# Expert outputs of the large tiles transposed by VectorE and scaled on ScalarE, in a fused FFT-convolution and mixture-of-experts kernel

## The chip, the cores and the metric

The kernel runs on one core of a Trainium2 chip. The metric is the device time of one launch in microseconds. Three runs of the kernel before took 2051.51, 2045.4 and 2051.67 us (median 2051.51). The profiled execution is another run: 2045.59 us, of which 2043.8 lie between its first and last instruction (the span).

Engine names in the rows: PE is TensorE (PEld its weight loads), DVE is VectorE, ACT is ScalarE, POOL is GpSimd, SP is SyncE, which here only issues DMAs. PEq, SPq, ACTq and POOLq are the sequencers of these engines.

## The reference

A causal convolution of every channel along the sequence by FFT, then a top-1 mixture of experts on the 45,568 rows that it gives:

```python
def _attn_ref(x, h):                      # x (8, 5696, 128), h (5696, 128)
    L = 2 * S
    Yf = np.fft.rfft(x, n=L, axis=1) * np.fft.rfft(h, n=L, axis=0)[None, :, :]
    return np.fft.irfft(Yf, n=L, axis=1)[:, :S, :].astype(np.float32)

def _moe_ref(x, modality_id, w_gate, modality_bias, w1, w2):   # 8 experts, 128 -> 1024 -> 128
    logits = x @ w_gate + modality_bias[modality_id]
    e_idx = np.argmax(logits, axis=1)
    probs = softmax(logits); gate_w = probs[np.arange(N), e_idx]
    for e in range(E):
        mask = e_idx == e
        h = np.maximum(x[mask] @ w1[e], 0.0)
        out[mask] = gate_w[mask, None] * (h @ w2[e])
```

## The kernel before

**Convolution.** `stage1` and `stage23` do the forward transform and the product with the filter in two groups of four batches; `stage4` does the last part of the inverse transform, computes the gate's logits and the place of each row in its expert's region, and puts (index, rows) on a queue. `dispatch` takes from that queue and GpSimd scatters 128 rows at a time to `rows_d` in device memory (L320): 128 values, the gate weight and the row's number in the output, 130 words a row. Each expert has its own region there.

**Expert tiles.** `Moe.tiles` works through 104 jobs: 81 large tiles of 512 rows (levels 0, 1 and 2 with 18, 18 and 45 tiles) and 23 small ones of 256 rows (level 3), the last three only if a count read on the chip asks for them; in the profiled run it didn't. Three weight slots are loaded from `w12s` when the expert of a slot changes (2 MB each, L613). A large tile has eight steps f, a small one four. Each step t, f does:
- `gemm1`: three matmuls of 512 columns (high and low parts of weights and rows), ScalarE's Relu into `hh` (L647), VectorE's rest into `hl` (L648);
- `gemm2`, two steps later (LAG = 2): three matmuls that add into `po`. With the last one, ScalarE copies `po` to `ot` (L669).

`load` (L603, L605) brings rows and their gate weight and row number (`mrt`, `mmt`) for the tile three ahead; for large tiles `mrt` comes in four DMAs with runs of 128 bytes, so that a VectorE transpose of 32x32 blocks (L626) completes the turning of the rows. `prep` makes the high and low parts (L629, L630) for the next tile at f = 4. `finish`, at f = 2 of the next tile, turns `ot` back: four TensorE transposes into the single bank `pxt` (L677), then VectorE multiplies with the gate weight into `of` (L680). The bank `pxt` also serves the transposes of the rows of small tiles (L622).

**Output.** 128 rows go out in one GpSimd scatter (a piece, L709). Tiles of levels 0 and 1 run while GpSimd is needed for `dispatch`; their outputs go to `late_d` (one DMA with rows of 2 KB, L684), and their row numbers are copied by GpSimd to `held` (L683). From tile 37 on, `bring` loads them again (L694). Pieces of levels 2 and 3 go out from `of` directly. `evenly` lets out at most one piece a step, 0.883 a step on the mean, each tied to that step's Relu; fresh pieces (`outs`) go ahead of brought ones (`backs`). What is left after the last tile is let out without a pace.

**Order.** While convolution and tiles run side by side (to about 1340 us), a scheduler sets the order on all engines but SP. In the last part, where tiles run alone (`alone`), TensorE's order is that of the code as well; ScalarE, VectorE and GpSimd keep the scheduler's. DMAs of SP and ACT take eight completion semaphores in turn: a DMA is issued only after the one eight places before it has landed.

**Tables.** `level` works out from the counts on which rows and expert each tile works. Level 2 and 3 are made together after the last `dispatch`; before them SP writes a padding of 512 rows behind each expert's region (L829).

Of the kernel before, what the change touches and what calls it, by code (L numbers as in the profile page):

```python
# [22 lines left out]
E, FF = 8, 1024  # L23
# [38 lines left out]
NHELD = LEVELS[0] + LEVELS[1]  # L62
SMALL = LEVELS[3] - NLAST
EVEN = ((NHELD + LEVELS[2]) * NSUB + SMALL * TSL // 128) / (8 * (LEVELS[2] - 2) + 4 * (SMALL - 3))
# [27 lines left out]
def conv_moe(  # L92
# [234 lines left out]
    def stage4(g, sp, ps, psl, qa, qb, paced=False, late=None):  # L327
# [39 lines left out]
        for q0 in range(qa, qb, QB):  # L367
# [7 lines left out]
            for qi in range(QB):  # L375
# [32 lines left out]
                else:  # L408
                    ys = [late.tile([128, GB, 128], BF16, name=f"ys{i}") for i in range(3)]
# [97 lines left out]
    def table(tp, lv, before):  # L507
# [26 lines left out]

        cnt = u_(E, "cnt")
# [8 lines left out]
        for s in range(3):  # L544
            nc.vector.tensor_tensor(sums[:, s + 1, E:], sums[:, s, E:], sums[:, s, E - (1 << s):2 * E - (1 << s)], op=ALU.add)
        cum = sums[:, 3, E - 1:]
# [8 lines left out]
        nc.vector.scalar_tensor_tensor(val[:, 1:], cum[:, :E], float(-ts), cur, op0=ALU.mult, op1=ALU.add)  # L555
        dlt = u_(E, "dlt")
# [3 lines left out]
        nc.vector.tensor_reduce(rb, ge, axis=AX.X, op=ALU.add)  # L560
        tmp = u_(nt, "tmp")
# [16 lines left out]
    class Moe:  # L578
        def __init__(self, wp, sp0, sp, pst, psh, pso):
# [3 lines left out]
            self.outs = []  # L583
            self.tabs = {}
            self.held = wp[0].tile([128, NHELD, NSUB], I32, name="held")
            self.back, self.backs, self.credit = 0, [], 0.0
# [4 lines left out]
        def load(self, t):  # L591
# [6 lines left out]
            mt = self.sp0.tile([128, NSUB, 2], F32, name="mmt", bufs=5)  # L598
# [6 lines left out]
            nc.sync.dma_start(mt[:, :ns], src[bass.ds(r0, ts), D:].rearrange("(c p) w -> p c w", p=128))  # L605
# [9 lines left out]
        def prep(self, t):  # L615
            st = self.st[t]
            rt, ts, ns = st["rt"], st["ts"], st["ns"]
            xp, s = (self.sp, "") if t else (self.sp0, "0")
            if self.on_pe(t):
# [3 lines left out]
                pf = px.rearrange("p c t -> p (c t)")[:, :ts]  # L623
            else:
                pf = self.sp0.tile([128, TS], F32, name="mxt", bufs=1)[:, :ts]
                nc.vector.transpose(pf, rt[:, :ts])  # L626
            xh = xp.tile([128, TS], F32R, name="mxh" + s)
            xl = xp.tile([128, TS], F32R, name="mxl" + s)
            nc.scalar.copy(xh[:, :ts], pf)  # L629
            nc.vector.tensor_tensor(xl[:, :ts], pf, xh[:, :ts].bitcast(F32), op=ALU.subtract)  # L630
            st.update(xh=xh[:, :ts], xl=xl[:, :ts])
# [19 lines left out]
        def gemm2(self, t, f):  # L651
# [15 lines left out]
            if k == 7:  # L667
                ot = self.sp.tile([128, TS], F32, name="ot")
                nc.scalar.copy(ot[:, :ts], po)  # L669
                st["ot"] = ot  # L670

        def finish(self, t):
            st = self.st.pop(t)
            ns = st["ns"]
            pq = self.pst.tile([128, NSUB, 128], F32, name="pxt")
            for c in range(ns):
                nc.tensor.transpose(pq[:, c, :], st["ot"][:, c * 128:(c + 1) * 128], ident)  # L677
            of = self.sp.tile([128, NSUB, D], F32, name="of")
            rt = st["mt"]
            nc.vector.tensor_tensor(of[:, :ns], pq[:, :ns], rt[:, :ns, 0:1].to_broadcast([128, ns, D]), op=ALU.mult)  # L680
            ri = rt.bitcast(I32)
            if t < NHELD:
                nc.gpsimd.tensor_copy(self.held[:, t, :].unsqueeze(2), ri[:, :, 1:])  # L683
                nc.sync.dma_start(late_d[t], of.rearrange("p c d -> p (c d)"))  # L684
                return
# [3 lines left out]
        def bring(self):  # L689
            if self.back < NHELD and len(self.backs) <= NSUB // 2:  # L690
                t = self.back
                self.back += 1
                of = self.sp.tile([128, NSUB, D], F32, name="ob")
                nc.sync.dma_start(of.rearrange("p c d -> p (c d)"), late_d[t])  # L694
                for c in range(NSUB):
                    self.backs.append((t, c, self.held[:, t, c:c + 1], of))
# [27 lines left out]
        def tiles(self, first, total):  # L724
# [11 lines left out]
            for g in range(len(steps) + LAG):  # L736
# [5 lines left out]
                if t < total:  # L742
# [3 lines left out]
                    if t > NHELD:  # L746
                        self.bring()
# [173 lines left out]
```

## Time and profile before

| | |
|---|---|
| runs | 2051.51, 2045.4, 2051.67 us |
| profiled execution | 2045.59 us, span 2043.8 us |
| TensorE busy | 1962.4 us, 96% |
| VectorE busy | 1445.8 us, 71% |
| ScalarE busy | 1133.6 us, 55% |
| GpSimd busy | 1112.3 us, 54% |

Four stages follow one another: the transforms up to about 800 us; the end of the inverse transform beside the tiles of levels 0 and 1 up to about 1340; large tiles alone up to about 1902; small tiles to the end. Busy time is the time in which at least one record of an engine is open. Matmuls overlap (one record of 512 columns lasts 0.39 us and the next begins 0.23 us after it), so the start-to-start distance, not the mean duration, tells what one costs.

### The profile page before, as it was taken

What the parts mean: (1) busy time and instruction counts of PE and PEld (TensorE: products, weight loads), DVE (VectorE), ACT (ScalarE), POOL (GpSimd) and SP (SyncE); (2) the same over time, 40 slices, a digit from 0 to 9 for tenths busy, and PEclk for the clock granted to TensorE, in tenths of its full rate; (3) what the DMA queues carried; (4) which work ended last, traced back from release to release, by engine and by line L of the source; (5) the groups of instructions that cost most, each with busy time, mean ns of one, the idle gap of its engine ahead of it and who ended that gap; (6) DMA issues with size and microseconds to landing.
All of it is one profiled execution on the core that took longest, in us unless ns stands there. A gap on an engine that the chain in (4) does not pass through costs nothing. (4 is left out here: it accounts for less than half of the span.)

```text
span 2043.8 us, 32620 instructions
## 1 busy us (share of the span) xinstructions
PE 1962.4 (96%) x9114; PEld 1418.1 (69%) x9114; DVE 1445.8 (71%) x2478; ACT 1133.6 (55%) x2000; POOL 1112.3 (54%) x1085
## 2 busy tenths in 40 slices
PE   6889999999999899899999999999999999999996
PEld 5755555544544445778878778788888888888996
DVE  7759888886787897577676776866666666666553
ACT  5756777644444444566566666555555555555553
POOL 2117777673777685444444444633555555555554
PEclk8989999999999998999999999999999999999998
DMA  9998999979999997644456644354333343334443
GB/s 332 403 354 286 330 325 326 299 237 325 331 336 322 308 328 240 187 133 133 104 168 173 177 125 101 80 173 92 78 77 78 79 116 81 76 80 150 149 152 121
DMA packets 395832, 407.09 MB, mean 199 GB/s; under 512 B 242584, under 2 KB 277369, under 8 KB 393345
## 3 DMA queue, kind: packets, MB, share of 16 engines
q1 hardware_dynamic: 324496, 271.97, 44.7%
q10 hardware_dynamic: 47920, 85.94, 13.1%
q0 software_dynamic: 23232, 47.08, 6.7%
q8 instruction: 74, 1.21, 0.2%
q14 instruction: 110, 0.89, 0.1%
HBM read 396.70 MB, written 182.99 MB: 284 GB/s over the span
## 5 line engine op out<-in xcount | busy, mean ns | idle before, releaser
L320 POOL DMA_INDIRECT rows<-rt,idx x360 | 369.2, 1025 | 271.1 <-ACT hh L647 184.0
L648 DVE SCALAR_TENSOR_TENSOR hl<-ph,hh 128x512 fp32r<-128x512 f32 x496 | 338.0, 684 | 211.7 <-ACT hh L647 205.7
L647 ACT ACTIVATE hh<-ph 128x512 fp32r<-128x512 f32 x496 | 295.7, 598 | 278.3 <-PE ph L644 234.1
L290 POOL TENSOR_TENSOR t<-t,t 96x512 f32<-96x512 f32 x224 | 328.7, 1487 | 140.5 <-DVE t L283 119.9
L283 DVE TENSOR_TENSOR t<-px,hs 96x512 f32<-96x512 f32 x512 | 318.2, 676 | 68.3 <-PE px L280 29.5
L709 POOL DMA_INDIRECT out<-of,mmt x220 | 216.8, 985 | 216.4 <-ACT hh L647 186.7
L664 PE MATMUL po<-hh,slot 128*128 128x512 f32 (+1 forms) x808 | 304.3, 377 | 7.0 <-ACT hh L647 6.9
L666 PE MATMUL po<-hl,slot 128*128 128x512 f32 (+1 forms) x808 | 300.3, 372 | 0.3 <-DVE hl L648 0.3
L665 PE MATMUL po<-hh,slot 128*128 128x512 f32 (+1 forms) x808 | 299.5, 371 | 0.0
L280 PE MATMUL px<-z,m 96*96 96x512 f32 x512 | 256.1, 601 | 5.7 <-DMA z<-z 2.7
L648 DVE SCALAR_TENSOR_TENSOR hl<-py,hh 128x512 fp32r<-128x512 f32 x232 | 160.0, 690 | 105.2 <-ACT hh L647 105.0
L647 ACT ACTIVATE hh<-py 128x512 fp32r<-128x512 f32 x232 | 138.5, 597 | 164.2 <-PE py L644 152.1
L263 ACT COPY ut<-pu 90x512 f32<-90x512 f32 x256 | 147.9, 580 | 137.2 <-PE pu L258 69.1
L642 PE MATMUL ph<-mxh,slot 128*128 128x512 f32 (+1 forms) x536 | 210.7, 393 | 4.6 <-SPq L720 3.8
L258 PE MATMUL pu<-t,mi 96*96 96x512 f32 x384 | 199.0, 610 | 7.9 <-ACT ut L263 4.6
L644 PE MATMUL ph<-mxl,slot 128*128 128x512 f32 (+1 forms) x536 | 201.9, 377 | 0.0
L643 PE MATMUL ph<-mxh,slot 128*128 128x512 f32 (+1 forms) x536 | 201.9, 377 | 0.0
L709 POOL DMA_INDIRECT out<-ob,held x144 | 139.9, 971 | 109.6 <-ACT hh L647 90.6
L664 PEld LDWEIGHTS po<-hh,slot 128*128 128x128 f32 x808 | 152.8, 189 | 35.2 <-ACT hh L647 9.8
L666 PEld LDWEIGHTS po<-hl,slot 128*128 128x128 f32 x808 | 152.5, 189 | 28.3 <-DVE hl L648 0.9
L665 PEld LDWEIGHTS po<-hh,slot 128*128 128x128 f32 x808 | 152.8, 189 | 25.1
L280 PEld LDWEIGHTS px<-z,m 96*96 96x96 f32 x512 | 82.4, 165 | 119.8 <-issue 72.9
(173 smaller groups left out, 3464.0 us busy)
## 6 DMA issues: line engine op xcount, KB each, us to landing
slot<-w12s SPq DMA_DIRECT2D x101, 2048.0 KB
z<-z SPq DMA_DIRECT2D x128, 360.0 KB
z<-z SPq DMA_DIRECT2D x45, 640.0 KB
z<-z SPq DMA_DIRECT2D x45, 512.0 KB
mrt<-rows SPq DMA_DIRECT2D x312, 64.0 KB
w12s<-ws ACTq DMA_DIRECT2D x32, 512.0 KB
u<-ua ACTq DMA_DIRECT2D x63, 256.0 KB
u<-ub ACTq DMA_DIRECT2D x63, 256.0 KB
```

The source lines that it names most:

```text
L280: nc.tensor.matmul(px[:KP], mm, zbuf[k % NZ][:, i], start=True, stop=True)
L283: prods[0] = nc.vector.tensor_tensor(prod[i, j].rearrange("p (b d) -> p b d", d=D), px[:KP].rearrange("p (b d) -> p b d", d=D), hs[:, j, k ...
L290: add = eng.tensor_tensor(y[:, i], y[:, i], prod[1, 1 - i], op=ALU.add if i else ALU.subtract)
L320: d = nc.gpsimd.indirect_dma_start(views[count[0] % NVIEW], bass.IndirectOffsetOnAxis(ap=idx[:, t:t + 1], axis=0), rt[:, t, :], None, boun ...
L642: nc.tensor.matmul(po, w[:, 0, 0, fs], st["xh"], start=True, stop=False)
L643: nc.tensor.matmul(po, w[:, 0, 1, fs], st["xh"], start=False, stop=False)
L647: st["act"] = nc.scalar.activation(hh, ph, AF.Relu)
L648: nc.vector.scalar_tensor_tensor(hl, ph, 0.0, hh.bitcast(F32), op0=ALU.max, op1=ALU.subtract)
L664: nc.tensor.matmul(po, w[:, 1, 0, fs], hh[:, cs], start=k == 0, stop=False)
L665: nc.tensor.matmul(po, w[:, 1, 1, fs], hh[:, cs], start=False, stop=False)
L666: nc.tensor.matmul(po, w[:, 1, 0, fs], hl[:, cs], start=False, stop=k == 7)
L709: d = nc.gpsimd.indirect_dma_start(oviews[(t * NSUB + c) % NVIEW], bass.IndirectOffsetOnAxis(ap=ix, axis=0), of[:, c, :], None, bounds_che ...
```

## The change

- A large tile's `po` is turned by VectorE (blocks of 32x32) into `ot`, which has two buffers for large tiles; the copy by ScalarE, the four TensorE transposes and VectorE's multiplication go. Four DMAs write `ot` to `late_d` in runs of 128 bytes, so that rows lie there in order.
- This holds for all 81 large tiles, level 2 included. `bring` loads each again, 2 KB a partition, into one of four buffers of `spare`, and `gate`, at least eight steps later, lets ScalarE multiply one piece a step with the gate weight in place. Gate weight and row number of all large tiles stay in `near` and `held`; the GpSimd copies go. Three sets of `ys` in `stage4` now lie in `spare`.
- Level 2's table is made after a fence; paddings and the table of level 3 are done in small parts (`later`) beside tiles from 39 on.
- A small tile's output transposes take the bank `pl` in place of `pxt`.
- In the last part ScalarE and VectorE keep the code's order too, and `prep` is spread over steps 3, 4 and 5 (0 and 1 in small tiles).

```diff
+NBIG = NHELD + LEVELS[2]
+NEAR = 4
+AGE = 7
+NOB = 4
...
-                    ys = [late.tile([128, GB, 128], BF16, name=f"ys{i}") for i in range(3)]
+                    h = qi % 2 * 3
+                    ys = [late[:, h + i] for i in range(3)]
...
-            self.outs = []
+            self.outs, self.later = [], iter(())
             self.tabs = {}
-            self.held = wp[0].tile([128, NHELD, NSUB], I32, name="held")
-            self.back, self.backs, self.credit = 0, [], 0.0
+            near = wp[0].tile([128, NEAR, NSUB, 2], F32, name="near")
+            held = sp.tile([128, NBIG - NEAR, NSUB, 2], F32, name="held", bufs=1)
+            self.spare = sp.tile([128, NOB, TS], F32, name="spare", bufs=1)
+            self.meta = [near[:, t] if t < NEAR else held[:, t - NEAR] for t in range(NBIG)]
+            self.back, self.ripe, self.backs, self.credit = 0, [], [], 0.0
...
-            mt = self.sp0.tile([128, NSUB, 2], F32, name="mmt", bufs=5)
+            mt = self.meta[t] if t < NBIG else self.sp0.tile([128, TSL // 128, 2], F32, name="mmt", bufs=8)
...
-            nc.sync.dma_start(mt[:, :ns], src[bass.ds(r0, ts), D:].rearrange("(c p) w -> p c w", p=128))
+            mv = src[bass.ds(r0, ts), D:]
+            nc.sync.dma_start(mt, mv.rearrange("(p c) w -> p c w", c=ns) if t < NBIG else mv.rearrange("(c p) w -> p c w", p=128))
...
-        def prep(self, t):
+        def turn(self, t):
...
+        def high(self, t):
+            st = self.st[t]
+            xp, s = (self.sp, "") if t else (self.sp0, "0")
+            st["xh"] = xp.tile([128, TS], F32R, name="mxh" + s)[:, :st["ts"]]
+            st["xl"] = xp.tile([128, TS], F32R, name="mxl" + s)[:, :st["ts"]]
+            nc.scalar.copy(st["xh"], st["pf"])
+
+        def low(self, t):
+            st = self.st[t]
+            nc.vector.tensor_tensor(st["xl"], st["pf"], st["xh"].bitcast(F32), op=ALU.subtract)
+
+        def prep(self, t):
+            self.turn(t)
+            self.high(t)
+            self.low(t)
...
-                ot = self.sp.tile([128, TS], F32, name="ot")
-                nc.scalar.copy(ot[:, :ts], po)
-                st["ot"] = ot
+                ot = st["ot"] = self.sp.tile([128, ts], F32, name=f"ot{ts}", bufs=ts // TSL)
+                if t < NBIG:
+                    nc.vector.transpose(ot, po)
+                else:
+                    nc.scalar.copy(ot, po)
 
         def finish(self, t):
             st = self.st.pop(t)
             ns = st["ns"]
-            pq = self.pst.tile([128, NSUB, 128], F32, name="pxt")
+            if t < NBIG:
+                for j in range(0, D, BK):
+                    nc.sync.dma_start(late_d[t].rearrange("(n p) d -> p n d", p=BK)[:, :, j:j + BK],
+                                      st["ot"][j:j + BK].rearrange("p (n w) -> p n w", w=BK))
+                return
+            pq = ps4l.tile([128, 2, 256], F32, name="pl").rearrange("p i (c t) -> p (i c) t", t=128)
             for c in range(ns):
                 nc.tensor.transpose(pq[:, c, :], st["ot"][:, c * 128:(c + 1) * 128], ident)
-            of = self.sp.tile([128, NSUB, D], F32, name="of")
+            of = self.sp.tile([128, TSL // 128, D], F32, name="of")
             rt = st["mt"]
-            nc.vector.tensor_tensor(of[:, :ns], pq[:, :ns], rt[:, :ns, 0:1].to_broadcast([128, ns, D]), op=ALU.mult)
+            nc.vector.tensor_tensor(of, pq[:, :ns], rt[:, :ns, 0:1].to_broadcast([128, ns, D]), op=ALU.mult)
             ri = rt.bitcast(I32)
-            if t < NHELD:
-                nc.gpsimd.tensor_copy(self.held[:, t, :].unsqueeze(2), ri[:, :, 1:])
-                nc.sync.dma_start(late_d[t], of.rearrange("p c d -> p (c d)"))
-                return
             for c in range(ns):
                 self.outs.append((t, c, ri[:, c, 1:2], of))
 
-        def bring(self):
-            if self.back < NHELD and len(self.backs) <= NSUB // 2:
-                t = self.back
+        def bring(self, t):
+            if self.back < min(NBIG, t - 1) and len(self.ripe) + len(self.backs) < (NOB - 1) * NSUB:
+                ob = self.spare[:, self.back % NOB].rearrange("p (c d) -> p c d", d=D)
+                nc.sync.dma_start(ob.rearrange("p c d -> p (c d)"), late_d[self.back].rearrange("(p c) d -> p (c d)", c=NSUB))
+                self.ripe += [[AGE, self.back, c, ob] for c in range(NSUB)]
                 self.back += 1
-                of = self.sp.tile([128, NSUB, D], F32, name="ob")
-                nc.sync.dma_start(of.rearrange("p c d -> p (c d)"), late_d[t])
-                for c in range(NSUB):
-                    self.backs.append((t, c, self.held[:, t, c:c + 1], of))
+
+        def gate(self, after=None):
+            for it in self.ripe:
+                it[0] -= 1
+            while self.ripe and (after is None or self.ripe[0][0] < 0):
+                _, t, c, ob = self.ripe.pop(0)
+                mt = self.meta[t]
+                m = nc.scalar.activation(ob[:, c], ob[:, c], AF.Copy, scale=mt[:, c, 0:1])
+                self.backs.append((t, c, mt.bitcast(I32)[:, c, 1:2], ob))
+                if after is not None:
+                    tc.add_manual_dep(m.ins, after.ins.name, PACED, reason="order")
+                    break
...
                     if t > NHELD:
-                        self.bring()
+                        self.gate(self.st[t]["act"])
+                        self.bring(t)
...
-                    if f == (4 if n == 8 else 0):
-                        self.prep(t + 1)
+                    parts = (self.turn, self.high, self.low)
+                    if not self.alone:
+                        if f == (4 if n == 8 else 0):
+                            self.prep(t + 1)
+                    else:
+                        for i, part in enumerate(parts):
+                            if f == (3 + i if n == 8 else min(i, 1)):
+                                part(t + 1)
                 if f == LAG and first <= t - 1:
                     self.finish(t - 1)
+                if self.alone and t > NHELD + 2 and f % 4 > 1:
+                    next(self.later, None)
...
-            while self.outs or self.backs or self.back < NHELD:
+            while self.outs or self.backs or self.ripe or self.back < NBIG:
                 self.scatter(len(self.outs))
+                self.gate()
                 self.outs, self.backs = self.backs, []
-                self.bring()
+                self.bring(total)
...
+            late = moe.spare.rearrange("p n t -> p (n t)").bitcast(BF16).rearrange("p (i b t) -> p i b t", b=GB, t=128)
+            s4 = stage4(0, sp4, ps4, ps4l, QA, NQ, late=late)
...
+            def after_all(padrow):
+                for e in range(E):
+                    r0 = nc.sync.value_load(padrow[0:1, e:e + 1], min_val=e * REGION, max_val=e * REGION + NTOK)
+                    nc.sync.dma_start(rows_d[bass.ds(r0, TS), :].rearrange("(p c) w -> p c w", c=NSUB), padt)
+                    yield
+                tab, ev[3] = yield from table(tp, 3, ev[2])
+                moe.tabs[3] = (tab, rows_d)
...
-                yield from stage4(1, sp4, ps4, ps4l, 0, NQ, late=sp)
+                yield from stage4(1, sp4, ps4, ps4l, 0, NQ, late=late)
...
-                for e in range(E):
-                    r0 = nc.sync.value_load(padrow[0:1, e:e + 1], min_val=e * REGION, max_val=e * REGION + NTOK)
-                    nc.sync.dma_start(rows_d[bass.ds(r0, TS), :].rearrange("(p c) w -> p c w", c=NSUB), padt)
-                level(2, rows_d)
-                level(3, rows_d)
+                fence()
+                level(2, views[NVIEW])
+                moe.later = after_all(padrow)
...
-            with tc.manual_schedule(engines={mybir.EngineType.PE}):
+            with tc.manual_schedule(engines={mybir.EngineType.PE, mybir.EngineType.Activation, mybir.EngineType.DVE}):
...
-    args.append(scratch("late", (NHELD, 128, TS)))
+    args.append(scratch("late", (NBIG, TS, D)))
```

TensorE's order where the output of tile 59 is turned (tiles alone; slot_7161 holds the weights of that tile, slot_7159 those of the next). Before:

```order
L666 MATMUL po<-hl,slot_7161 128x512
L642 MATMUL ph<-mxh,slot_7159 128x512
L643 MATMUL ph<-mxh,slot_7159 128x512
L644 MATMUL ph<-mxl,slot_7159 128x512
L664 MATMUL po<-hh,slot_7159 128x512
L665 MATMUL po<-hh,slot_7159 128x512
L666 MATMUL po<-hl,slot_7159 128x512
L677 MATMUL pxt<-ident,ot 128x128 x4
L642 MATMUL py<-mxh,slot_7159 128x512
```

After, the same place:

```order
L689 MATMUL po<-hl,slot_7161 128x512
L665 MATMUL ph<-mxh,slot_7159 128x512
L666 MATMUL ph<-mxh,slot_7159 128x512
L667 MATMUL ph<-mxl,slot_7159 128x512
L687 MATMUL po<-hh,slot_7159 128x512
L688 MATMUL po<-hh,slot_7159 128x512
L689 MATMUL po<-hl,slot_7159 128x512
L665 MATMUL py<-mxh,slot_7159 128x512
```

The four transposes are gone and nothing stands in their place; all else is in the same order.

ScalarE's order after, with large tiles alone (`spare` is a brought tile, one row a gated piece of it). Before, the same stretch has eight Relus, one `mxh` and one copy of `ot` to a tile.

```order
L670 ACTIVATE hh<-ph 128x512
L728 ACTIVATE spare<-spare,held 128x128
L670 ACTIVATE hh<-py 128x512
L728 ACTIVATE spare<-spare,held 128x128
L670 ACTIVATE hh<-ph 128x512
L728 ACTIVATE spare<-spare,held 128x128
L645 CAST mxh<-mxt 128x512
L670 ACTIVATE hh<-py 128x512
```

Nearly every Relu now has a gated piece behind it.

GpSimd's last scatters ahead of the count that decides on the last three tiles (`of` are pieces of small tiles; `ob` before and `spare` after are brought pieces). Before:

```order
L709 DMA out<-of,mmt 45568x128 x3
L709 DMA out<-ob,held 45568x128
L709 DMA out<-of,mmt 45568x128
L709 DMA out<-ob,held 45568x128 x2
L709 DMA out<-of,mmt 45568x128 x4
L719 TENSOR_LOAD tab_15729
```

After:

```order
L745 DMA out<-spare,held 45568x128
L745 DMA out<-of,mmt 45568x128 x2
L745 DMA out<-spare,held 45568x128 x3
L745 DMA out<-of,mmt 45568x128 x2
L745 DMA out<-spare,held 45568x128 x2
L755 TENSOR_LOAD tab_16795
```

The last four pieces of `of` stand together before; after, three brought pieces stand between the two pairs and two behind them.

## Rows read from the trace of the kernel before

**Rows 1.** Page: busy tenths in 40 slices; DMA is the share of 16 DMA engines.

```profile
PE   6889999999999899899999999999999999999996
...
PEclk8989999999999998999999999999999999999998
DMA  9998999979999997644456644354333343334443
```

**Rows 2.** Windows: us, busy (instructions) of PE, PEld, DVE, ACT, POOL, clock, DMA share, GB/s.

```profile
840.00:1340.00 500.00, 498.11 (x2730) 400.82 (x2730) 362.54 (x784) 311.94 (x562) 247.75 (x290) 1.00 0.50 135
1400.00:1900.00 500.00, 500.00 (x2272) 410.50 (x2271) 313.39 (x477) 256.23 (x435) 284.16 (x291) 1.00 0.38 90
```

**Rows 3.** Timeline of PE, 1604 to 1606 us: start, duration, line, instruction.

```profile
1604.88 0.39 PE L666 MATMUL po<-hl,slot 128*128 128x512 f32 x1
1605.11 0.60 PE L677 MATMUL pxt<-ident,ot 128*128 128x128 f32 x4
1605.46 0.48 PE L642 MATMUL py<-mxh,slot 128*128 128x512 f32 x1
1605.78 0.39 PE L643 MATMUL py<-mxh,slot 128*128 128x512 f32 x1
1606.01 0.39 PE L644 MATMUL py<-mxl,slot 128*128 128x512 f32 x1
```

**Rows 4.** Source line L677, whole span: count, duration ns min/median/max, starts, shape.

```profile
L677 PE MATMUL pxt<-ident,ot x364: 270/272/329, 841.6 to 2031.0; 128*128 128x128 f32 x182
```

**Rows 5.** Lines of PE, 840 to 1340 us: count, busy us, mean ns, idle before.

```profile
L677 PE MATMUL pxt<-ident,ot 128*128 128x128 f32 x124 | 18.6, 272 | 0.0
```

**Rows 6.** Lines by form, 1400 to 1900 us: count, busy us, mean ns, idle before.

```profile
L648 DVE SCALAR_TENSOR_TENSOR hl<-py,hh 128x512 fp32r<-128x512 f32 x175 | 120.7, 690 | 74.9 <-ACT hh L647 74.9
...
L680 DVE TENSOR_TENSOR of<-pxt,mmt 128x512 f32<-128x512 f32 x44 | 29.9, 680 | 0.0
...
L626 DVE STREAM_TRANSPOSE mxt<-mrt 128x512 f32<-128x512 f32 x41 | 28.8, 702 | 1.4 <-DMA mrt<-rows 1.4
L629 ACT CAST mxh<-mxt 128x512 fp32r<-128x512 f32 x42 | 26.1, 621 | 22.8 <-PE py L643 22.8
...
L669 ACT COPY ot<-po 128x512 f32<-128x512 f32 x43 | 25.2, 587 | 4.0
```

**Rows 7.** Lines by form, ACT, 795 to 1345 us.

```profile
L451 ACT ACTIVATE ex<-lg 128x96 f32<-128x96 f32 x19 | 5.5, 290 | 1.0 <-DVE lg L436 0.9
```

**Rows 8.** Waits, 795 to 845 us: engine, line, releaser, us in total, times, longest.

```profile
ACT hh L647 <- DMA slot<-w12s: 9.4, 1, 9.4
...
PE po L664 <- ACT hh L647: 6.8, 1, 6.8
```

**Rows 9.** Waits of ACT, 840 to 1340 us.

```profile
ACT hh L647 <- DMA slot<-w12s: 6.7, 2, 4.5
```

**Rows 10.** DMA, 1400 to 1900 us: queue, packets, MB, share of 16 engines.

```profile
q1 hardware_dynamic: 114454, 25.46, 27.0%
```

**Rows 11.** Waits of SP's queue, 1400 to 1900 us.

```profile
SPq L613 <- PE po L666: 230.9, 43, 7.8
SPq L694 <- DMA out<-ob,held: 10.1, 8, 2.4
```

**Rows 12.** Timeline of SP, 1604 to 1607 us.

```profile
1604.79 1.96 SPq L603 DMA_DIRECT2D mrt<-rows  x4
```

**Rows 13.** Chain that ended last, in order of time: start, us, what.

```profile
1964.31 8.22 DMA slot<-w12s
```

**Rows 14.** Lines by form, DVE, 1305 to 1320 us.

```profile
L545 DVE TENSOR_TENSOR sums<-sums 1x8 f32<-1x8 f32 x6 | 0.9, 158 | 0.1
```

**Rows 15.** Timeline of POOL, 2029 to 2044 us.

```profile
2030.36 0.97 POOL L709 DMA_INDIRECT out<-of,mmt  x1 [0.30 <-issue]
2032.05 0.97 POOL L709 DMA_INDIRECT out<-of,mmt  x1 [0.72 <-DVE of L680]
2033.33 0.97 POOL L709 DMA_INDIRECT out<-of,mmt  x1 [0.30 <-issue]
```

More of the change, by code (lines that the diff above doesn't have):

```diff
@@ L62 @@
 NHELD = LEVELS[0] + LEVELS[1]
+NBIG = NHELD + LEVELS[2]
+NEAR = 4
+AGE = 7
+NOB = 4
 SMALL = LEVELS[3] - NLAST
-EVEN = ((NHELD + LEVELS[2]) * NSUB + SMALL * TSL // 128) / (8 * (LEVELS[2] - 2) + 4 * (SMALL - 3))
+EVEN = (NBIG * NSUB + SMALL * TSL // 128) / (8 * (LEVELS[2] - 2) + 4 * (SMALL - 3))
 JOBS = [(lv, j) for lv, n in enumerate(LEVELS) for j in range(n)]
@@ L545, in table @@
             nc.vector.tensor_tensor(sums[:, s + 1, E:], sums[:, s, E:], sums[:, s, E - (1 << s):2 * E - (1 << s)], op=ALU.add)
+        yield
         cum = sums[:, 3, E - 1:]
@@ L555, in table @@
         nc.vector.scalar_tensor_tensor(val[:, 1:], cum[:, :E], float(-ts), cur, op0=ALU.mult, op1=ALU.add)
+        yield
         dlt = u_(E, "dlt")
@@ L560, in table @@
         nc.vector.tensor_reduce(rb, ge, axis=AX.X, op=ALU.add)
+        yield
         tmp = u_(nt, "tmp")
@@ L613, in load_weights @@
             nc.sync.dma_start(self.slots[t % NSLOT].bitcast(F32), w12s[bass.ds(ex, 1)].rearrange("o p a i f -> (o p) a i f"), cond=ch > 0)
-        def prep(self, t):
+        def turn(self, t):
             st = self.st[t]
             rt, ts, ns = st["rt"], st["ts"], st["ns"]
-            xp, s = (self.sp, "") if t else (self.sp0, "0")
             if self.on_pe(t):
@@ L622, in prep @@
                     nc.tensor.transpose(px[:, c, :], rt[:, c * D:(c + 1) * D], ident)
-                pf = px.rearrange("p c t -> p (c t)")[:, :ts]
+                st["pf"] = px.rearrange("p c t -> p (c t)")[:, :ts]
             else:
-                pf = self.sp0.tile([128, TS], F32, name="mxt", bufs=1)[:, :ts]
+                pf = st["pf"] = self.sp0.tile([128, TS], F32, name="mxt", bufs=1)[:, :ts]
                 nc.vector.transpose(pf, rt[:, :ts])
[L627 to L631, printed above, removed]
+        def high(self, t):
[11 more added lines that the diff above has]
+            self.low(t)
         def gemm1(self, t, f):
@@ L805, in level @@
             def level(lv, src):
-                tab, ev[lv] = table(tp, lv, ev[lv - 1])
+                g = table(tp, lv, ev[lv - 1])
+                while True:
+                    try:
+                        next(g)
+                    except StopIteration as done:
+                        tab, ev[lv] = done.value
+                        break
                 moe.tabs[lv] = (tab, src)
-            s4 = stage4(0, sp4, ps4, ps4l, QA, NQ, late=sp)
+            late = moe.spare.rearrange("p n t -> p (n t)").bitcast(BF16).rearrange("p (i b t) -> p i b t", b=GB, t=128)
+            s4 = stage4(0, sp4, ps4, ps4l, QA, NQ, late=late)
             for _ in range(AHEAD):
@@ L814, in conv_moe @@
                 level(0, views[NVIEW])
+            def after_all(padrow):
+                for e in range(E):
+                    r0 = nc.sync.value_load(padrow[0:1, e:e + 1], min_val=e * REGION, max_val=e * REGION + NTOK)
+                    nc.sync.dma_start(rows_d[bass.ds(r0, TS), :].rearrange("(p c) w -> p c w", c=NSUB), padt)
+                    yield
+                tab, ev[3] = yield from table(tp, 3, ev[2])
+                moe.tabs[3] = (tab, rows_d)
             def rest():
```

## Prediction

> **What bounds the kernel now.** I read the page's slices first, then windows by stage, then the order of time on TensorE, then who waits for whom. From the third slice on TensorE is busy eight or nine tenths of nearly every slice, at the full granted clock from 850 us until just before the end [rows 1]. In the two stages in which tiles run, it is busy 498.1 of 500 us and 500.0 of 500 us, while VectorE has 363 and 313, ScalarE 312 and 256, GpSimd 248 and 284, and the DMA engines half or less [rows 2]. The reader is to see that nothing else is near full there. A busy engine is not yet the bound, since matmul records overlap. So I look at starts: 0.23 us from one matmul of 512 columns to the next, without a hole, also where a tile ends [rows 3]. VectorE, before its part of the hidden layer, is idle because it waits for ScalarE's Relu [rows 6], and ScalarE waits for TensorE, but for 6.7 us of waits for DMAs [rows 9]. So TensorE sets the pace from about 840 us on, and what leaves its row shortens the run, as long as the others keep up.
>
> **What goes from TensorE.** In [rows 3] the last matmul before the four output transposes starts at 1604.88 and the second one after them at 1605.78: 0.90 us, where two steps of 0.23 would be 0.46. The four transposes so cost 0.44 us in place (not the 4 x 0.272 that their records last). There are 364 transposes of this line [rows 4]; 40 of them belong to the 20 small tiles and stay, 324 belong to 81 large tiles and go. 81 x 0.44 = 35.6 us. 124 of them lie in 840 to 1340 us [rows 5]: 31 tiles with 13.6 us of it; the other 50 tiles have 22.0.
>
> **What comes to VectorE and ScalarE.** On VectorE the transpose of `po` takes the place of the multiplication. A transpose that reads PSUM is not in the trace; its neighbours are the multiplication out of PSUM, 0.680 us, and the transpose out of SBUF, 0.702 us [rows 6]. I take 0.70: 0.02 us more a tile, on an engine that has 4 us a tile to spare. The transpose stands behind the hidden part of step f = 1, where VectorE now has 0.69 + 0.70 = 1.39 us in a step of 6 x 0.23 = 1.38; the next step has 0.69 alone, so nothing adds up. ScalarE loses a copy of 0.587 a large tile and gets 0.883 gated pieces a step, 7.1 a tile. A piece of 128x128 out of SBUF is not in the trace. Bounds are 0.290 for 128x96 [rows 7] and 0.621 for 128x512 [rows 6]; on the line between them 128 columns cost 0.32, which I take. ScalarE then has 8 x 0.60 + 0.62 + 7.1 x 0.32 = 7.7 us of work in a tile of 11.0; with 0.621 each it would be 9.8. Both fit. Cover: VectorE's result is wanted two steps and two matmuls after its input (2 x 1.38 + 0.46 = 3.2 us), the Relu and VectorE take 0.60 + 0.69 and I estimate 0.3 for handing over, so ScalarE may be about 1.6 us late before TensorE feels it. I cost both at 0.
>
> **The new wait.** A gated piece stands in ScalarE's fixed order and waits for its load. Behind it stand the next Relus, and TensorE behind these. The load is issued eight steps earlier, 8 x 1.38 = 11.0 us. On SP it waits for the scatters of the buffer's former pieces; such waits were 8 before, at most 2.4 us [rows 11]. SP also issues four more DMAs a tile, 2.0 us by the four of `mrt` [rows 12]; it waited for TensorE 230.9 us in 43 tiles, 5.4 us each [rows 11], so these and one more load have room. With a wait of 2.4, 2.0 of issues and 1.1 of transfer (next part) I estimate that a load lands some 6 us after its place in the order. The worst neighbour is a weight slot, 8.22 us to land [rows 13]: behind one, a load may come in 2 to 3 us late, of which 1.6 is covered. A handful of these happen; I put 0 on them in the sum, and 5 us in the range.
>
> **DMA engines.** SP's queue has 114,454 packets in 500 us at 27.0% of 16 engines [rows 10], 18.9 ns a packet. The output of a tile makes 2,048 packets of 128 bytes: 2,048 x 18.9 / 16 = 2.4 us, 22% of a tile of 11.0. A brought tile moves 256 KB; at the stretch's 90 GB/s for 38% [rows 2] that is 1.1 us or 10%, and there are 45 more of them. 0.38 + 0.22 + 0.10 = 0.70, which is not full. In the mixed stage a tile takes 500 / 31 = 16 us, so 15% come to 50%, less the wide writes that go. Writes of 128 bytes to device memory are not in the trace; the price is that of reads mostly of this size. The Trainium skill (DMA: Bandwidth & Descriptors, Specifications) says that transfers under 512 bytes make the DMA engine read, modify and write; no run here shows a store of that size. If that doubled the price of these packets (an estimate), the share with tiles alone would be 0.92, and landings would be late more often; this is the second rival's weight, not a term of the sum.
>
> **The mixed stage.** ScalarE also issues loads of the inverse transform here, and takes its turn in the same eight DMA semaphores as SP. Where SP's transfers are slow, ScalarE stands still: 9.4 us once at the start of the tiles, of which TensorE lost 6.8 [rows 8], and 6.7 us later in two waits [rows 9]. Three more DMAs a tile turn the wheel faster. Bounds: 0, or two more stops of 6.8, which is the whole 13.6. I take 3, nearer to what [rows 9] cost TensorE, which is almost nothing [rows 2].
>
> **The end.** The start of bringing costs eight steps in which no piece goes out, and this comes back at the end: five brought pieces now stand between or behind the last four small ones in GpSimd's order. A piece takes 1.28 us from start to start [rows 15]. 5 x 1.28 = 6.4, less the 0.42 us that GpSimd waited there beyond the usual 0.30 [rows 15]: +6.0 us, on the path, since the last scatter ends the run.
>
> **The rest.** Level 3's table goes into VectorE's fixed order; its heaviest part has seven small operations like the additions of 0.158 [rows 14], 1.1 us in a step that has 0.69 already. With the next step that is 0.4 us over, within the 1.6; I put 1 us on all parts. The other PSUM bank in small tiles frees nothing that TensorE waits for; the paddings leave a place where TensorE was busy. Both 0, and so the GpSimd copies.
>
> **Sum.** -35.6 + 0 + 3 + 6.0 + 1 = -25.6 us. From the profiled execution, 2045.59, that gives 2020. Two of the three runs lie 6 us above it, and the median is 2051.51; against it I predict 2026.
>
> **Rivals.**
> - The mixed stage gives nothing back: ScalarE's DMA waits eat the 13.6. For it [rows 8], against it [rows 9]. -35.6 + 13.6 + 6.0 + 1 = -15: 2036.5.
> - The brought loads come late, everywhere: ScalarE stands before the gate at each of the 81 loads. It decides from landings later than 11.0 + 1.6 us. If each is 0.7 us beyond that, TensorE loses 57 us, and -25.6 + 57 gives 2083. For it speak the fixed order and the fuller DMA engines, against it that SP idles most of a tile [rows 11] and that the worst transfer seen takes 8.22 us [rows 13].
> - Some of each: half the loads behind a slot or the table's parts hold TensorE for 20 to 25 us in all, and nothing changes: 2048.
> - Better than the sum: the pause of 6.8 us at the start [rows 8] falls away with the GpSimd copies and ScalarE's lighter row, 2017.
>
> **How the numbers follow.** What a measurement can tell from no change is 0.3%, 6.2 us. Chances: the sum 0.61, better 0.06, the mixed stage 0.17, nothing 0.08, late loads 0.08. Faster so has 0.84, same 0.08, slower 0.08. The forecast's own range is 2014 to 2037. The whole range goes from 2012 (the lower level of the runs, 2045.4, with 33 us off) to 2046, which takes in the mixed rival and leaves out the slow one.
>
> **What would show it.** Right: no L677 group of 512 columns' tiles, 0.23 us from matmul to matmul across the tile's end, a large tile in 11.0 us where it was 11.4; ScalarE's pieces near 0.32 us and hardly waiting for a DMA; the VectorE transposes near 0.70; the last scatter about 8 us behind the last transpose in place of 2.3 [rows 4, 15]. Wrong: holes on TensorE that end with the Relu, ScalarE waiting for `spare` loads or for weight slots, DMA shares above 0.9, or a mixed stage as long as before.

## The result, and the profile after

On the chip of the trace before, the changed kernel takes 2022.32 us (median of four runs, 2021.18 to 2026.85) against 2051.47 us (four runs, 2045.4 to 2051.67): ratio 0.9877, 95% interval 0.9859 to 0.9895. The forecast was 2026. The profiled execution took 2021.57 us with a span of 2019.8, 24.0 us less than the profiled one before; the sum had said 25.6. (Against the medians the gain is 29.2 us: the profiled execution before was itself 5.9 us under its median.)

Page of the kernel after, 40 slices [rows 1]:

```profile
PE   6889999999999998899999999999999999999995
...
PEclk9989999999999998999999999999999999999998
DMA  9998999979999997665566655355766666667543
```

Windows of the kernel after, columns as in [rows 2]:

```profile
840.00:1340.00 500.00, 496.20 (x2637) 396.41 (x2637) 361.79 (x764) 301.31 (x537) 253.95 (x265) 0.99 0.58 140
1400.00:1900.00 500.00, 499.60 (x2303) 414.11 (x2302) 334.00 (x522) 357.36 (x717) 293.67 (x300) 1.00 0.66 148
```

TensorE is as full as before. The counts of the second window (2303 after, 2272 before) can't be held against each other, because after the change the last 28 us of it are small tiles with shorter matmuls; from 1400 to 1860 us, large tiles alone in both, TensorE is busy in all 460 us of both kernels. DMA rose from 0.38 to 0.66 (estimated: 0.70), also from 1400 to 1860. In the mixed stage TensorE lost 3.8 us to holes (before 1.9), and its mean granted clock was 0.99 where it was 1.00.

TensorE at the end of a large tile, kernel after [rows 3]; the last matmul of the tile starts at 1604.76:

```profile
1604.53 0.40 PE L688 MATMUL po<-hh,slot 128*128 128x512 f32 x1
1604.76 0.39 PE L689 MATMUL po<-hl,slot 128*128 128x512 f32 x1
1604.99 0.39 PE L665 MATMUL py<-mxh,slot 128*128 128x512 f32 x1
1605.22 0.40 PE L666 MATMUL py<-mxh,slot 128*128 128x512 f32 x1
```

Nothing stands between two tiles any more: 0.23 us from one start to the next. A large tile takes 10.93 to 11.18 us from result to result, where it took 11.38 to 11.60.

Lines by engine of the kernel after, 1400 to 1880 us [rows 6]: count, busy us, mean ns, idle before:

```profile
L728 ACT ACTIVATE spare<-spare,held 128x128 f32<-128x128 f32 x282 | 113.6, 403 | 9.6 <-DMA spare<-late 0.5
...
L693 DVE STREAM_TRANSPOSE ot<-po 128x512 f32<-128x512 f32 x43 | 30.4, 706 | 0.0
L638 DVE STREAM_TRANSPOSE mxt<-mrt 128x512 f32<-128x512 f32 x42 | 29.5, 702 | 0.0
```

The transpose out of PSUM costs 0.706 us (taken: 0.70), a gated piece 0.403 (taken: 0.32, bounds 0.29 and 0.62), and the gate waited for loads 0.5 us in all.

Where the 24 us come from is read from the starts of the operation that takes `po` away (`ot<-po`), tile by tile:

| stretch | before | after | gained | predicted |
|---|---|---|---|---|
| up to the 1st result | 839.4 | 838.8 | 0.6 | 0 |
| 1st to 33rd (mixed stage) | 511.5 | 504.4 | 7.1 | 13.6 - 3 |
| 33rd to 81st (large tiles alone) | 551.6 | 528.8 | 22.8 | 22.0 - 1 |
| 81st to 101st (small tiles) | 128.0 | 125.6 | 2.4 | 0 |
| 101st to the end of the span | 13.3 | 22.2 | -8.9 | -6.0 |

The 22.0 in the third row was worked out for 50 tiles; 48 lie in this stretch, 21.1 us by the same price.

### The profile page after: what moved, and what is told of

The parts are those of the page before. It is cut to its first block, busy times and chain, and to the rows that moved or that the text cites. A ratio compares the mean times of both kernels' runs of the same rounds, so it can differ in the third digit from the quotient of the medians.

```text
span 2019.8 us, 32681 instructions
## 1 busy us (share of the span) xinstructions
PE 1928.1 (95%) x8790; PEld 1385.7 (69%) x8790; DVE 1451.5 (72%) x2478; ACT 1212.1 (60%) x2243; POOL 1114.2 (55%) x1050
## 4 chain that ended last, share of the span: by engine, by line
PE 54%; DMA 4%; issue 2%; DVE 2%; POOL 1%; ACT 1%; SPq 0%; ACTq 0%; POOLq 0%; DVEq 0%
PE po L687 8%; PE po L688 8%; PE po L689 8%; PE ph L665 5%; PE ph L667 5%; PE ph L666 5%; PE py L397 3%; PE py L665 3%; PE py L667 3%; PE py L666 3%; DMA slot<-w12s 2%; PE pl L411 1%; DMA mrt<-rows 1%; PE py L404 1%; DMA rows<-rt,idx 1%
## 5 line engine op out<-in xcount | busy, mean ns | idle before, releaser
L324 POOL DMA_INDIRECT rows<-rt,idx x360 | 376.3, 1045 | 301.0 <-ACT hh L670 224.1
L745 POOL DMA_INDIRECT out<-spare,held x308 | 302.0, 981 | 206.1 <-ACT hh L670 187.8
L728 ACT ACTIVATE spare<-spare,held 128x128 f32<-128x128 f32 x308 | 124.0, 403 | 10.5 <-DMA spare<-late 0.5
```

The source lines that it names most:

```text
L324: d = nc.gpsimd.indirect_dma_start(views[count[0] % NVIEW], bass.IndirectOffsetOnAxis(ap=idx[:, t:t + 1], axis=0), rt[:, t, :], None, boun ...
```

## The same two kernels on other chips

The experiments ran on four other chips, and there the gain was smaller or gone. Each time is a median of device us, with the number of runs:

| chip | before | changed | ratio, 95% interval |
|---|---|---|---|
| first (the prediction's) | 2051.47 (4) | 2022.32 (4) | 0.9877, 0.9859 to 0.9895 |
| second | 2062.44 (16) | 2050.47 (9) | 0.994, 0.9916 to 0.9963 |
| third | 2064.46 (9) | 2054.15 (6) | 0.9943, 0.9924 to 0.9961 |
| fourth | 2068.71 (20) | 2070.38 (12) | 1.0021, 1.0002 to 1.004 |

The run of the changed kernel on the second chip:

> The changed kernel as it is, once more on the chip of the other three runs, so that they can be held against it: about 2022, ratio 0.986 to 0.989.

It was 28 us slower than on the first. To see whether the chip or the change does this, the third chip ran both kernels:

> The kernel before as it is, for a trace of it from the chip of the other three runs. In the runs so far the changed kernel gained 29 us on one chip and 12 on another, where its trace shows ScalarE standing still for 1 to 3 us some 34 times in 460 us, at Relus whose matmuls were long done. Theory (these pauses belong to the chip and come with every kernel): this one has as many, but hides them. Rival (they come from the change, the gated pieces or the fuller DMA engines): it has none, as on the first chip.

> The changed kernel as it is, on the chip of the other three runs: 2022 on a chip like the first, 2050 on one like the second; 12 to 29 us below the kernel before.

Waits of ScalarE, 1340 to 1900 us, of the kernel before on the third chip ("issue": the engine stood, and the profile shows nothing that it waited for), and one register move of SP's queue there (ns min/median/max):

```profile
ACT hh L647 <- issue: 36.9, 51, 0.9
...
L603 SPq MOVE mrt<-rows x164: 2/29/709, 1405.0 to 1865.9; - x164
```

The same of the changed kernel on the first chip, which has no "issue" row:

```profile
ACT hh L670 <- PE ph L667: 86.3, 196, 1.0
ACT hh L670 <- PE py L667: 73.6, 156, 1.0
...
L615 SPq MOVE mrt<-rows x156: 29/29/29, 1409.3 to 1833.0; - x156
```

And on the third:

```profile
ACT hh L670 <- issue: 34.7, 82, 1.2
ACT spare L728 <- DMA spare<-late: 12.8, 3, 6.0
...
L615 SPq MOVE mrt<-rows x164: 2/29/702, 1400.2 to 1863.5; - x164
```

On the first chip a register move takes 29 ns nearly every time (at most 37 in the kernel before); on the others the median is 29 too, but single moves take up to 0.7 us, on the third chip in both kernels. I call this, and ScalarE's standing still, pauses; what holds the instructions up is not shown. The kernel before has them too, in its one trace from the third chip: the theory that they come with the chip holds, and the rival falls. But that kernel hides them: nearly all its large tiles take 11.37 to 11.60 us there, as on the first chip. Windows 1400 to 1900 us on the third chip, first before, then changed:

```profile
1400.00:1900.00 500.00, 500.00 (x2270) 410.29 (x2269) 313.09 (x478) 255.24 (x436) 281.94 (x287) 1.00 0.38 89
```

```profile
1400.00:1900.00 500.00, 491.95 (x2114) 394.87 (x2113) 319.00 (x506) 335.82 (x687) 280.78 (x286) 0.99 0.63 139
```

From the 34th to the 81st result, the kernel before takes 539.5 us on the first chip and 542.0 on the third. The changed one takes 518.0 on the first, and 534.8, 535.0 and 544.6 on the second, third and fourth. In the profiled executions of the third chip the change gains 8.6 us where it gained 24.0 on the first; from the 33rd to the 81st result it gains 7.7 where it gained 22.8, so the missing gain is there. (7.3 more are missing before the first result, where no large tile has ended yet, and the other stages gain more than on the first chip.) What TensorE's weight loads wait for in the changed kernel on the third chip, from the 34th to the 81st result, covers the 17.0 us by which this stretch is longer than on the first chip, where no such wait is listed:

```profile
PEld po L687 <- ACT hh L670: 12.2, 11, 4.4
PEld po L689 <- DVE hl L671: 5.7, 17, 0.4
```

A pause, in the timeline of the changed kernel on the second chip:

```profile
1568.92 0.60 ACT L670 ACTIVATE hh<-py 128x512 fp32r<-128x512 f32 x1 [0.20 <-PE py L667]
...
1569.89 0.39 PE L667 MATMUL ph<-mxl,slot 128*128 128x512 f32 x1
...
1572.42 0.60 ACT L670 ACTIVATE hh<-ph 128x512 fp32r<-128x512 f32 x1 [2.90 <-PE py L667]
...
1573.05 0.40 ACT L728 ACTIVATE spare<-spare,held 128x128 f32<-128x128 f32 x1
1573.35 0.58 ACT L670 ACTIVATE hh<-py 128x512 fp32r<-128x512 f32 x1
```

After a pause in the kernel before, third chip:

```profile
1567.70 0.60 ACT L647 ACTIVATE hh<-py 128x512 fp32r<-128x512 f32 x1 [2.10 <-PE py L644]
1568.22 0.60 ACT L647 ACTIVATE hh<-ph 128x512 fp32r<-128x512 f32 x1
```

The Relu at 1572.42 reads a `ph` that was done at 1570.28; the named releaser is not its cause. After such a pause the changed kernel puts a gated piece behind each Relu and needs 0.93 us for the two (1572.42 to 1573.35), so of each step of 1.38 us it makes up 0.45; the kernel before has a Relu alone (0.52 us from start to start, 1567.70 to 1568.22) and makes up 0.86. That this sets the loss is argued from these times; the run with the pieces on VectorE below bears on it. The worst place, third chip:

```profile
1447.97 2.15 SPq L872 DMA_DIRECT2D rows<-padt  x2
...
1450.28 0.33 SPq L718 DMA_DIRECT2D spare<-late  x1
...
1453.33 0.40 ACT L728 ACTIVATE spare<-spare,held 128x128 f32<-128x128 f32 x1 [6.01 <-DMA spare<-late]
...
1454.78 0.50 PE L687 MATMUL po<-hh,slot 128*128 128x512 f32 x1 [3.97 <-ACT hh L670]
```

Here a moved padding stands in SP's queue ahead of a brought load; the load is issued at 1450.28, the gate waits 6.0 us, TensorE 4.0. Three windows there (columns as in [rows 2]) show that the granted clock, a mean of stretches at 2.4 and at 1.2 GHz, then falls as well:

```profile
1445.00:1449.00 4.00, 4.00 (x19) 3.31 (x18) 3.79 (x16) 2.00 (x5) 3.09 (x4) 1.00 0.74 131
1449.00:1453.00 4.00, 1.81 (x8) 1.05 (x6) 0.55 (x1) 0.00 (x0) 0.29 (x1) 1.00 0.71 236
1453.00:1458.00 5.00, 3.22 (x9) 2.31 (x10) 3.17 (x9) 4.17 (x9) 1.96 (x2) 0.81 0.56 161
```

On the first chip the paddings go out between 1415.7 and 1433.8 us, also ahead of loads, and the gate waits at most 0.32 us. So the padding alone does not make a load late, and a second late load has none ahead of it (SP took 5.70 us there to issue four DMAs of `mrt`, where 1.96 is usual [rows 12]):

```profile
1861.06 0.40 ACT L728 ACTIVATE spare<-spare,held 128x128 f32<-128x128 f32 x1 [4.57 <-DMA spare<-late]
1862.51 0.80 PE L687 MATMUL po<-hh,slot 128*128 128x512 f32 x1 [2.58 <-ACT hh L670]
```

From the 34th to the 81st result TensorE stood idle 7.8 us on the third chip; 6.6 of it are these two places, and the clock fell behind both (0.66 from 1862 to 1867 us). I estimate from such windows that late loads cost about 10 of the 17 us lost on the second and on the third chip, and a third of the 27 on the fourth; I put the rest down to the pauses. So two things failed there, not one: loads that came after their gate, and ScalarE's room to catch up.

## Experiments

**The transposes put back** (second chip).

```
+ pq = self.pst.tile([128, NSUB, 128], F32, name="pxt")
+ for c in range(ns):
+     nc.tensor.transpose(pq[:, c, :], st["ot"][:, c * 128:(c + 1) * 128], ident)
```

> The changed kernel, with four TensorE transposes of the finished tile put back into each of the 81 large tiles; their result is used by nobody. Theory (the four transposes in TensorE's row are the whole gain): the tiles alone lose 0.44 to 0.475 us each again, 22 to 23 us in 49 tiles, and the mixed stage its 7.5 us or more; about 2052 to 2056, above the kernel before, since the longer end stays. Rival (part of the gain comes from ScalarE, which no longer copies the large tiles out of PSUM, or from the new order of steps): the tiles alone get back less than 0.3 us each, and the time stays under 2040.

2079.48 us (6 runs), 29 above the changed kernel of the same chip and ratio 1.0068 to the one before (1.0045 to 1.0092). From the first to the 29th result it falls 10.9 us behind, and by the last result it is 28.7 behind. An undisturbed tile takes 11.6 to 11.8 us instead of 10.9 to 11.2. TensorE at the end of a tile:

```profile
1608.44 0.39 PE L689 MATMUL po<-hl,slot 128*128 128x512 f32 x1
1608.78 0.66 PE L703 MATMUL pxt<-ident,ot 128*128 128x128 f32 x4
...
1609.51 0.40 PE L666 MATMUL py<-mxh,slot 128*128 128x512 f32 x1
```

The theory holds: TensorE's row is the gain, and the other parts of the change, which this run keeps, don't bring it. Its price was expected otherwise, though: here the four cost 0.6 to 0.7 us a tile (1.07 us from 1608.44 to 1609.51, less two steps of 0.23), since they also wait for VectorE's `ot`. And from the 33rd to the 81st result the run is only 18.3 us behind, 0.38 a tile: no wait of TensorE's weight loads for the Relu is listed in it any more, where the changed kernel on this chip has 10.6 us. That fits a longer row on TensorE that hides the pauses, as in the kernel before.

**A faster pace of the scatters** (second chip).

```
- EVEN = (NBIG * NSUB + ...
+ EVEN = 1.03 * (NBIG * NSUB + ...
```

> The pace of the scatters is 3% higher, nothing else. Counted by the code's rule, the changed kernel has eight brought pieces left behind its last step, this one none. Theory (the 8.9 us that the end gave back are pieces left over): the last scatter stands about 3 us behind the last small tile's result in place of 11.1, and the time falls by 6 to 8 us, to about 2015. Rival (the last load or GpSimd's own row bounds the end): within 2 us of the changed kernel, 2020 to 2024.

2051.83 us (6 runs), no less than the changed kernel's 2050.47: the rival's number, but not its reason. The end did shrink by about what the theory said, from 19.6 us (start of the last small tile's result to the end of the span) to 13.3, but the stretch from the 34th to the 81st result grew from 534.8 to 543.1. Why it grew is open.

**The small-row DMAs of the mixed stage taken away** (second chip).

```
+ if t < NHELD:
+     nc.sync.dma_start(late_d[t].rearrange("(p c) d -> p (c d)", c=NSUB), st["ot"])
+     return
```

> For the 32 tiles of the first two levels the four DMAs of 128-byte rows that write a tile's result are replaced by one of 2 KB rows; the rows and columns of these tiles so come out in other places. Theory (these DMAs are why the mixed stage gave only 7.5 us where its transposes are worth 13.6: they delay the rows that ScalarE and TensorE wait for): the stage from the first tile's result to the 33rd's gets 3 to 6 us shorter, the time is 2016 to 2019. Rival (the stops come from weight slots and the inverse transform's own loads, whatever the result's DMAs do): the stage within 1.5 us of the changed kernel's, 2021 to 2024.

2052.81 us (8 runs). First to 33rd result: 512.7 us, where the changed kernel took 515.6 on this chip and 511.1 on the third. That is 2.9 us less than on its own chip, where 3 to 6 were expected, but inside the spread of the two chips, and nothing of it is seen in the time, with 71,000 packets less. The theory isn't borne out. (This version leaves out that rows must come out in their places.)

**The gate two steps behind its load** (third chip).

```
- AGE = 7
+ AGE = 1
```

> The changed kernel, with the gated piece of a brought tile placed two steps behind its load instead of eight, 2.8 us instead of 11.0. Theory (the gate stands in ScalarE's fixed order, and only the distance of eight steps keeps it free): at many of the 81 loads ScalarE now waits 2 us or more, 1.6 of it is covered, and TensorE loses 0.5 to 3 us at each; the time grows by 40 us or more over the changed kernel. Rival (the scheduler's place in the order or the load's speed leave room anyway): within 6 us of the changed kernel.

2166.52 us (4 runs), 112 above the changed kernel beside it. Waits of ScalarE, 1340 to 1900 us:

```profile
ACT spare L728 <- DMA spare<-late: 175.0, 51, 7.7
```

The distance of eight steps is what keeps the gate free, as the theory had it (40 us or more).

**The gated pieces on VectorE** (third chip, then fourth).

```
- m = nc.scalar.activation(ob[:, c], ob[:, c], AF.Copy, scale=mt[:, c, 0:1])
+ m = nc.vector.tensor_scalar(ob[:, c], ob[:, c], mt[:, c, 0:1], None, op0=ALU.mult)
```

> The gated pieces are multiplied by VectorE instead of ScalarE, everything else as in the changed kernel. Theory (with 7.1 pieces of 0.40 us a tile ScalarE has too little room to make up for its pauses, and the holes on TensorE come from there): on a chip with the pauses the tiles alone get 8 to 15 us shorter, on one without nothing. Rival (the pauses themselves are longer than any slack, or VectorE, with 0.69 us of each 1.38 taken, becomes late instead): within 4 us of the changed kernel or slower.

2035.41 us (4 runs), ratio 0.9863 (0.9834 to 0.9892): a gain as large as on the first chip, 19 us under the changed kernel beside it. From the 34th to the 81st result it takes 522.3 us against 535.0, 12.7 less, inside the 8 to 15 expected. Another 8.4 us of the difference between the two profiled executions lie before the first tile's result, where no gated piece runs yet; those aren't explained. Its windows, 1400 to 1900 us, and the waits of TensorE's weight loads from the 34th to the 81st result:

```profile
1400.00:1900.00 500.00, 499.06 (x2235) 406.96 (x2234) 380.49 (x819) 237.50 (x407) 289.73 (x296) 1.00 0.65 146
...
PEld po L689 <- DVE hl L671: 3.9, 12, 0.4
PEld po L687 <- ACT hh L670: 1.4, 4, 0.6
```

The gate, now on VectorE, waited for loads 3.0 us in all (12.8 on ScalarE in the changed kernel), so late loads were also shorter in this run, and part of the 12.7 us is theirs.

A second time, beside the changed kernel on the fourth chip:

> The changed kernel as it is, beside the next two runs: 2022 on a chip on which the engines don't pause, 2050 to 2054 on one on which they do; so far 2022 on one chip, 2050 and 2054 on two.

> The gated pieces on VectorE, once more. Theory (ScalarE's lack of room against pauses cost the changed kernel some 15 to 20 us on the second and third chip): on a chip with pauses again 15 to 20 us under the changed kernel, about 2035; on a chip without, the same as it within 3 us, 2019 to 2025. Rival (the pieces on VectorE are better for another reason, or it was chance): under the changed kernel by 10 us or more on any chip, or not at all.

The changed kernel took 2070.38 us, more than any number expected; the pieces on VectorE 2056.37 (9 runs), ratio 0.994 (0.9918 to 0.9961), 14 us less, where 15 to 20 were expected. The stretch is 531.5 against 544.6. So twice 13 us of it go with the pieces. The rival (VectorE is the better place for another reason, on any chip) stays open, since no chip without pauses ran this version.

**Both together** (fourth chip).

> The gated pieces on VectorE, and a pace of the scatters that is 3% higher. Theory (the two add up: in the run with the faster pace the end after the last small tile's result was 13.3 us instead of 19.6): 5 to 8 us under the run with the pieces on VectorE alone, 2028 on a chip with pauses, 2014 on one without. Rival (the faster pace makes the tiles as much longer as it makes the end shorter, as it did with the pieces on ScalarE): within 3 us of it.

2050.78 us (6 runs), ratio 0.9926 (0.9902 to 0.9949). It is the fastest on this chip, 5.6 us under the version with the pieces alone, but the intervals of the two overlap, so the theory isn't shown: in the profiled executions it is 7.2 us longer from the 34th to the 81st result and 3.7 shorter at the end.

**Three steps of cover in place of two** (fifth chip).

```
- LAG = 2
+ LAG = 3
```

> The changed kernel, gated pieces on ScalarE, with one number changed: the second matmuls of a step are issued three steps behind the first ones instead of two, so that ScalarE and VectorE have 1.38 us more before TensorE feels that they are late. Theory (on the chips with pauses the changed kernel lost 17 to 27 us of the stage of tiles alone because ScalarE was late by more than the 1.6 us that two steps cover): from the 34th to the 81st tile's result it takes 518 to 524 us, where it took 518.0 on the chip without pauses and 534.8, 535.0 and 544.6 on those with them. Rival (the pauses stop TensorE's own row, or the weight slots and loads, which now stay in use a step longer, set the time): 530 us or more there.

2072.03 us (12 runs; the kernel before 2067.99, ratio 1.0015, 0.9995 to 1.0034); the stretch took 541.7 us, the rival's side. The changed kernel itself did not run on this chip. Waits of TensorE in the stretch:

```profile
PE ph L665 <- ACT mxh L645: 8.1, 2, 7.3
PE ph L667 <- DVE mxl L649: 4.7, 5, 1.0
```

No wait for `hh` is left; the next tile's input, which comes from the same two engines and was not moved, is late in its place. And the gate still waits (23.5 us, 7 times): the wait of 7.3 us comes right behind a gate that stood 10.35 us for a late load, and the granted clock was 0.58 from 1462 to 1472 us. Without that place the stretch would lie near the rival's bound (541.7 less 7.3 and the clock's 4.2, an estimate of 530), so this run says little on the theory. It shows that more distance for one of ScalarE's results was not enough.

## Why the prediction came out right, and where it does not hold

The sum said 25.6 us and the profiled executions differ by 24.0. The mechanism and the largest term were right; that the rest came so close is in part luck: the mixed stage and the end came out 3.5 and 2.9 us worse than their terms, large tiles, small tiles and the start 1.8, 2.4 and 0.6 better.

- **TensorE's row.** 0.44 us a tile in place was predicted, 22.8 / 48 = 0.475 came (0.45 between undisturbed tiles); the transposes put back cost it again. Right.
- **The mixed stage.** Term +3, measured 13.6 - 7.1 = 6.5: less than half of it was put down. Its bounds were 0 and 13.6. ScalarE waited for rows, and TensorE behind it, which made most of the holes of 3.8 us. Right behind the two longest, in 1054 to 1062 and 1157 to 1166 us, the granted clock was 0.79 and 0.81 (means of stretches at 2.4 and 1.2 GHz), an estimated 1.7 us of loss each, where before it was 1.00 over the whole stage [rows 2]. Holes (1.9 more than before) and clock (3.4) make 5.3 of the 6.5 us. Waits of ScalarE and TensorE, 840 to 1340 us, after [rows 9]:

```profile
ACT yt L407 <- DMA mrt<-rows: 8.9, 2, 5.7
ACT rt L400 <- DMA rows<-rt,idx: 7.3, 6, 1.9
...
PE py L404 <- ACT rt L400: 1.8, 3, 1.3
PE pl L411 <- ACT yt L407: 1.4, 1, 1.4
```

  The clock was not in the sum. That the small writes are the cause isn't borne out; what delays these rows stays open.
- **DMA engines.** 0.66 for 0.70. The doubled price that the second rival weighed isn't seen. DMA queue after, 1400 to 1900 us [rows 10]:

```profile
q1 hardware_dynamic: 214101, 53.57, 53.6%
```

  That is 0.536 x 500 x 16 / 214101 = 20.0 ns a packet against 18.9 before, over packets of all sizes. The traces hold each packet: from 1400 to 1860 us those of 128 bytes took 14.0 ns on the mean before (80,915 of them, all loads of rows) and 13.7 after (169,037, half of them the new stores). So the price of 18.9 was too high for these, and the stores took 16% of a tile, not 22. The Trainium skill (DMA: Bandwidth & Descriptors, Specifications) has transfers under 512 bytes read, modified and written; these packet times show no extra cost of it.
- **The end.** Term +6.0, measured 8.9. GpSimd after, the last scatters [rows 15]:

```profile
1998.37 0.98 POOL L745 DMA_INDIRECT out<-of,mmt  x1 [0.30 <-issue]
1999.66 0.98 POOL L745 DMA_INDIRECT out<-spare,held  x1 [0.31 <-issue]
2000.95 0.98 POOL L745 DMA_INDIRECT out<-spare,held  x1 [0.30 <-issue]
2003.56 0.98 POOL L745 DMA_INDIRECT out<-spare,held  x1 [1.62 <-DMA out<-of,mmt]
2004.84 0.98 POOL L745 DMA_INDIRECT out<-of,mmt  x1 [0.30 <-issue]
```

  The five pieces were counted rightly; a wait of 1.62 us for an earlier scatter (L745 at 2003.56), 1.3 more than the usual 0.30, came on top. Of the other 1.6 us of the difference 0.6 lie behind the last scatter; the rest isn't located.
- **Small tiles.** 0 predicted, 2.4 gained: TensorE's waits there were 4.8 us before (one of 3.8) and 3.2 after; why is not shown. The other PSUM bank was not tried by itself.
- **ScalarE and the gate at nothing.** On the first chip this held (0.5 us of waits), though a piece took 0.403 and not 0.32. On the three other chips that ran it this was the step that failed: I asked whether ScalarE's mean work fits its tile (7.7 of 11.0 us), and took one covering time of 1.6 us (in which the 0.3 for handing over is from no row). A pause of 2 us exceeds that, and what is left of a step sets how fast it is made up. Late loads were put at nothing in the sum too, by a longest transfer of 8.22 us, though the chain that it was read from has one of 9.11 at 1151.75 us; on those chips gates waited up to 6.6 us. 17 to 27 us were lost from the 34th to the 81st result, and 2050, 2054 and 2070 us lie outside the forecast's whole range, near the rival in which nothing changes.

## What to carry to other kernels

When work moves to an engine that feeds the bound, count not only whether it fits, but how fast that engine makes up for a pause: here 0.45 us a step where it was 0.86. Of two engines with room, try it on the one from which the bound does not wait first (14 and 19 us on the two chips tried); a fixed-order wait needs its distance (eight steps here, two cost 112 us). Measure a change of one per cent on more than one chip.

## What was not expected of the hardware

- Register moves of SP's queue take 29 ns (at most 37) in the first chip's traces and 2 to 731 ns in the others', with pauses of ScalarE up to some 3 us. The cause stays open.
- A 128x128 multiplication by a value per row takes 403 ns on ScalarE and 276 ns on VectorE (median, third chip).
- After TensorE was busy only 1.81 of 4 us, its granted clock was 0.81 in the next 5 (third chip), a mean of 2.4 and 1.2 GHz.
- A packet of a 128-byte store took no longer than one of a 128-byte load (13.7 ns for both mixed, 14.0 for loads alone).
